# Two tiles taken in turn by halves of the weights, and another order of the first loads

## The chip, the cores and the metric

The kernel runs on one core of a Trainium2 chip. The metric is the device time of the whole program in microseconds (us), as the median of several runs. A core has a matrix engine (TensorE, PE in the rows, with its weight loads as PEld), a vector engine (VectorE, DVE), a scalar engine (ScalarE, ACT), a general engine (GpSimd, POOL) and a sync engine (SyncE, SP). They run side by side and wait for each other by semaphores; each takes its own instructions in order. Here SP issues nearly all DMA transfers, and POOL issues those that store attention's results and those that add what they bring to what is there. SBUF is the memory on the chip from which the engines work, PSUM holds what PE sums up, in banks of 128 x 512 fp32 values, and DRAM is the memory outside.

## What is computed

Three layers follow one another: linear attention with a norm (8 batches, 8 heads, 576 positions, 64 values a head), a first feed-forward layer with squared ReLU, and a second one with g = h·cos(h). The tokens are 8 x 576 = 4608, the model width is 512, the inner width 2048.

```
kv  = einsum('bhsd,bhse->bhde', k, v);  out = einsum('bhsd,bhde->bhse', q, kv)
x   = out / sqrt(mean(out*out, -1) + 1e-6) * g_norm          # heads side by side: 4608 x 512
x   = relu(x @ w_in)**2 @ w_out                              # first layer
out = (h * cos(h)) @ w2_out, with h = x @ w2_in              # second layer
```

The weights come as 64-bit numbers, and the kernel builds its own 32-bit values from their two words. Every large product is made of three: a value is split into a high part that PE's fast fp32 form keeps exactly and a low part, and high·high, high·low and low·high are added.

## The kernel before

**Tiles and chunks.** The first layer is done in two ways. One half of its inner width (8 weight blocks of 128, `NH`) goes through `layer_in` and `layer_out` for 9 tiles of 512 tokens (`NTILE`); this is the first stage, to about 495 us. The other half of the first layer and the whole second one follow in `run_slots`, in a scheme with seven products in place of eight on blocks of four, and its results are added to those of the first stage. A chunk is one tile with one weight block: `layer_in(t, f)` makes the 128 x 512 first products in 12 matmuls (L383), `act_relu2` squares and splits them (ACT at L392, L394 and L397, DVE at L398), and `layer_out(t, f)` makes 12 matmuls (L420) into four accumulators `acc0` to `acc3`, one for each 128 output columns, over all weight blocks of the tile. `layer_out` comes two chunks behind `layer_in` (`LAG`). Behind a tile's last weight block `evict` copies the four accumulators to SBUF, two by ACT (L406) and two by DVE (L408), and SP stores the pairs to DRAM in `p_d` (L409). The order of chunks is a plain list (L682): all eight blocks of tile 0, then all eight of tile 1, and so on.

**Attention runs beside the chunks.** For each batch: five loads of k and v (`load_kv`, L247), 80 small matmuls (`kv_mm`, L259), a copy to `kvx` (L272), and then eight units, two for each of four pairs of heads: `att_a` (PE at L292 for the first two batches, in full fp32, at L296 for the others; ACT at L303 and L304), `att_b` (PE at L318 or L320, ACT at L323 and L325), `att_c` (DVE at L333, L334, L335) and, for the first two batches, `att_d`, which writes the split result straight into the tiles 0 and 1 (ACT at L352, DVE at L353). Tile 0 is tokens 0 to 511, all from batch 0; tile 1 is 512 to 1023, the rest of batch 0 and most of batch 1. `att_e` stores the results, from where the later tiles are loaded.

**Weights.** `load_w` brings one half of a block (half 0 is of w_in, half 1 of w_out; 512 KB) and `conv_steps` turns it into high and low parts: DVE at L111, L113, L116, L122, L125 and L206, ACT at L112 and L205. Eight blocks make 16 conversions.

**What sets the order.** Each job has a position on a line that counts chunks (`at`, `run_jobs`), negative ones come before the first chunk. The 16 conversions stand at -14 to -13.7 (blocks 0 and 1), from -2.2 in steps of 0.7 (blocks 2 to 5) and from 4 in steps of 0.8 (blocks 6 and 7). Batch 0's units start at -13, one for each step of 1, batch 1's at -3 in steps of 0.8. `att_b`, `att_c` and `att_d` follow at 1.5 behind. The jobs are issued in the order of their positions, and a planner under the language then orders each engine's instructions by its own reckoning of when they are ready, with that order as the priority. Loads go ahead in streams: the first are issued by hand (L898 to L903): two weight halves, five tiles of k and v, one weight half, four of q, one weight half; after that each conversion issues the load of a later one (`Stream.place`), as soon as a buffer is free.

**Sums.** In the second stage, `load_sum` (L588) loads the first stage's results from `p_d` as the start of the first layer's sums, and `drain_product` adds the second half's products from PSUM (L670).

Of the kernel before, what the change touches and what calls it, by code (L numbers as in the profile page):

```python
# [8 lines left out]
F32 = mybir.dt.float32  # L9
# [4 lines left out]
ALU = mybir.AluOpType  # L14
PSUM = bass.MemoryType.PSUM

P = 128
# [5 lines left out]
def kernel(  # L23
# [15 lines left out]
    nc = tc.nc  # L39
    NT, DM = out.shape  # L40
    NKC = DM // P
    NF = wA.shape[0]
    NH = NF // 2
# [3 lines left out]
    NRAW = 4  # L47
# [5 lines left out]
    TOK = 512  # L53
    NTILE = NT // TOK
# [11 lines left out]
    dram = ctx.enter_context(tc.tile_pool(name="dram", bufs=1, space=bass.MemoryType.DRAM))  # L66
# [4 lines left out]
    zerob = cpool.tile([P, 1], F32, name="zerob")  # L71
    expb = cpool.tile([P, 1], F32, name="expb")

    x_d = [dram.tile([P, NKC, S], F32, name=f"x_d{b}") for b in range(B)]
    p_d = [dram.tile([P, NKC, TOK], F32, name=f"p_d{t}") for t in range(NTILE)]
    y_d = [dram.tile([P, 2, NKC, ht], F32, name=f"y_d{t0}") for t0, ht in TILES]
    first_pair = (NP, 0)
    groups_of = [range(NP // 2), range(NP)]
# [25 lines left out]
    wts = {}  # L104
# [60 lines left out]
    def conv_steps(kind, m, f, i):  # L165
        raw = raws.pop((kind, m, f, i))
        if kind in ("pair", "seven", "pairs"):
            n = 2 * P if kind == "pairs" else P
            w, e = words(raw, [P, 4, n])
# [7 lines left out]
            if where:  # L177
                size = 1024 // n
# [20 lines left out]
        w, e = words(raw, [P, DM])  # L199
        wf = as32(w[:])  # L200
        value(raw, wf, w, e)
        if i == 0:
            wts[m, f] = [w_p.tile([P, 2, DM], F32R, tag="w", name=f"w{x}") for x in "hl"]
        h, l = (x[:, i, :] for x in wts[m, f])
        nc.scalar.copy(out=h, in_=wf)  # L205
# [192 lines left out]
        nc.vector.tensor_tensor(out=l, in0=g, in1=as32(h[:]), op=ALU.subtract)  # L398
        return h, l

    def evict(t, i, acc):
        if i % 2 == 0:
            evs[t, i // 2] = ev_p.tile([P, 2, 512], F32, tag="ev", name="ev")
        both = evs[t, i // 2]
        if i % 2 == 0:
            nc.scalar.copy(out=both[:, 0, :], in_=acc)  # L406
        else:
            nc.vector.tensor_copy(out=both[:, 1, :], in_=acc)  # L408
            nc.sync.dma_start(out=p_d[t][:, i - 1:i + 1, :], in_=both)  # L409

    def layer_out(t, f):
        wh, wl = (x[:, 1, :] for x in wts[0, f])
        gh, gl = gs.pop((t, f))
        for i in range(NKC):
            if f == 0:
                accs[i] = bank_tile(f"acc{i}")
            o = accs[i]
            cs = slice(i * P, (i + 1) * P)
            for n, (a, m) in enumerate(((wh, gh), (wh, gl), (wl, gh))):
                nc.tensor.matmul(  # L420
                    o, a[:, cs], m[:], start=(f == 0 and n == 0), stop=(f == NH - 1 and n == 2), skip_group_check=True
                )
            if f == NH - 1:
                evict(t, i, o)


    slots = [(m, t, q) for m in range(2) for t in range(len(TILES)) for q in groups_of[m]]
# [155 lines left out]
    def load_sum(k, d, j):  # L583
        m, t, q = slots[k]
        t0, ht = TILES[t]
        sums[m, t, d, j] = e = w_p.tile([P, 2, 512], F32, tag="w", name="sum")
        for b, s0, done, size in pieces(t0 + j * ht, ht, TOK):
            nc.sync.dma_start(out=e[:, :, done:done + size], in_=p_d[b][:, 2 * d:2 * d + 2, s0:s0 + size])  # L588

    def s_block(k, i):  # L590
        m, t, q = slots[k]
# [87 lines left out]

    chunks = [(t, f) for t in range(NTILE) for f in range(NH)]  # L682
    nA0 = NTILE * NH
    nAtt = 49
    LAG2 = 1.25
# [35 lines left out]
        return [(kind, m, p, i) for p in ps for i in range(2)]  # L721

    w_items, w_at = [], []
    for fs, n, step in ((range(2), -14, 0.1), (range(2, 6), -2.2, 0.7), (range(6, NH), 4, 0.8)):
        new = [("one", 0, f, i) for f in fs for i in range(2)]
        w_items += new
        w_at += [n + step * k for k in range(len(new))]
    for new, n0, n1 in (
# [12 lines left out]
    late_stream.place([pos(n) for n in (0.95, 2.5, 3.25, 4.5, 6.4, 8.3, 11.3)], 0, lead=0.5)  # L741

    kv_stream = Stream(load_kv, kv_mm, [(b, c) for b in range(B) for c in range(NSC)])
    starts = [(-13, 1), (-3, 0.8)] + [(-3 + 7 * (b - 1), 7 / (2 * NKC)) for b in range(2, B)]
    kv_stream.place([s0 - 0.5 for s0, _ in starts for c in range(NSC)], 0)
    q_items = [(b, p) for b in range(B) for p in range(NKC)]
    q_next = NKC
# [138 lines left out]
    with ExitStack() as early:  # L886
        pools["ps"] = early.enter_context(tc.tile_pool(name="ps0", bufs=1, space=PSUM))
        def right(name, bufs):
            return early.enter_context(tc.tile_pool(name=name, bufs=bufs, side="right"))

        right("pad", 1).tile([P, 56], F32, name="pad")
        ev_p, pools["raw"] = right("ev", 2), right("conv", 2)
        x_p, g_p, pools["t"] = (right(n, b) for n, b in (("x", XB), ("g", 3), ("tmp", 8)))
        with tc.tile_pool(name="att", bufs=1, side="right") as att_p:
            kvx = [att_p.tile([P, NKC, P], F32, tag=f"kvx{b}", name=f"kvx{b}") for b in range(2)]
            for x in kvx:
                nc.gpsimd.memset(x, 0.0)
            w_stream.advance(2)  # L898
            kv_stream.advance(KVB)
            w_stream.advance(1)  # L900
            for p in range(NKC):
                load_q(0, p)
            w_stream.advance(NRAW - 3)  # L903
            run_jobs(-1)
            banks.update(o=["o", "acc3"], ss=["ss"], l=["l0", "l1"])
            run_chunks(0, nAtt)
        pools["x"] = ctx.enter_context(tc.tile_pool(name="xb", bufs=13, side="left", reuse_waits="tile"))
        banks["l"] = ["l0", "l1", "o", "ss"]
        run_chunks(nAtt, nA0)
        for c in chunks[-LAG:]:  # L910
            layer_out(*c)
# [48 lines left out]
```

## Time and profile before

| what | value |
| --- | --- |
| median of 3 runs | 1559.48 us (1559.1 to 1560.09) |
| the profiled execution's own time | 1560.63 us |
| its span, first to last instruction | 1558.8 us |
| PE busy | 1533.3 us, 98% of the span |
| DVE busy | 1294.2 us, 83% |
| ACT busy | 1077.1 us, 69% |
| POOL busy | 109.8 us, 7% |
| DMA | 426.71 MB, 274 GB/s on average |

The profile is of one execution. An engine's busy time is the union of its instructions' records. A matmul's record is longer than the time to the next matmul's start, since they are pipelined. In the rows, L383 is line 383 of the kernel, `out<-in` names the tiles written and read, and a bracket tells how long the engine was idle before and what ended that. The granted clock of TensorE was 1.00 in all stretches read here.

### The profile page before, as it was taken

The numbers are of one execution on the slowest core, as the hardware profiler recorded it, in microseconds if no ns is written. First come the engines' busy times: TensorE is split into PE (matmuls) and PEld (weight loads), VectorE is DVE, ScalarE is ACT, GpSimd is POOL, SyncE is SP. The second block draws the span as 40 slices with busy tenths as digits, with TensorE's granted clock in tenths as the row PEclk, the third lists the DMA queues.
The fourth block names the chain that finished last, engine by engine and source line by source line (L and its number), as shares of the span: only waits on it lengthen the run. The fifth ranks groups of instructions, "written<-read, shape, count | busy, mean of one in ns | idle before, by whom it ended". The sixth has DMA issues, their size and how long they took to land.

```text
span 1558.8 us, 24668 instructions
## 1 busy us (share of the span) xinstructions
PE 1533.3 (98%) x9104; PEld 1345.9 (86%) x9104; DVE 1294.2 (83%) x1743; ACT 1077.1 (69%) x1529; POOL 109.8 (7%) x173
## 2 busy tenths in 40 slices
PE   6999999999999999999999999999999999999998
PEld 4677777778888888888998899999999999999998
DVE  6987888888886899989889979867986788779777
ACT  6977777775444765656556777776777677777775
POOL 1112111110000000000000000000000000000001
PEclk9999999999999999999999999999999999999999
DMA  9748889777678989898999788887888789999996
GB/s 337 270 149 244 276 283 275 222 214 214 206 226 298 325 253 367 299 380 267 364 339 372 265 281 255 249 285 215 254 247 284 215 247 273 298 326 292 301 311 171
DMA packets 222295, 426.71 MB, mean 274 GB/s; under 512 B 18016, under 2 KB 138080, under 8 KB 222176
## 3 DMA queue, kind: packets, MB, share of 16 engines
q1 hardware_dynamic: 210400, 390.13, 72.8%
q0 software_dynamic: 11616, 35.01, 10.6%
q8 instruction: 73, 1.20, 0.3%
q14 instruction: 46, 0.38, 0.1%
q10 hardware_dynamic: 160, 0.00, 0.0%
HBM read 317.72 MB, written 81.79 MB: 256 GB/s over the span
## 4 chain that ended last, share of the span: by engine, by line
PE 87%; DVE 5%; DMA 3%; ACT 2%; issue 2%; SPq 0%; POOL 0%; DVEq 0%; ACTq 0%; POOLq 0%
PE FB L509 16%; PE FA L509 16%; PE SA L642 16%; PE SB L642 15%; PE acc L420 11%; PE l L383 9%; PE o L383 1%; PE ss L383 1%; DMA xraw<-x_d 1%; DMA sum<-part 1%; PE o L259 1%; DMA ws_d<-raw 1%; DMA kvld<-in_kv 1%; DVE gl L619 1%; PE l L259 1%
## 5 line engine op out<-in xcount | busy, mean ns | idle before, releaser
L509 PE MATMUL FB<-xh,wi 128*128 128x512 f32 (+1 forms) x840 | 301.4, 370 | 0.0
L509 PE MATMUL FA<-xh,wi 128*128 128x512 f32 (+1 forms) x840 | 301.4, 370 | 0.0
L642 PE MATMUL SB<-ws,gh 128*128 128x256 f32 x1008 | 233.0, 280 | 0.6 <-ACT part L667 0.6
L642 PE MATMUL SA<-ws,gh 128*128 128x256 f32 x1008 | 233.2, 280 | 0.0
L642 PEld LDWEIGHTS SA<-ws,gh 128*128 128x128 f32 x1008 | 183.7, 188 | 12.8 <-issue 0.5
L642 PEld LDWEIGHTS SB<-ws,gh 128*128 128x128 f32 x1008 | 183.3, 188 | 12.6 <-ACT part L667 0.8
L509 PEld LDWEIGHTS FB<-xh,wi 128*128 128x128 f32 x840 | 157.2, 188 | 9.6
L509 PEld LDWEIGHTS FA<-xh,wi 128*128 128x128 f32 x840 | 157.1, 188 | 9.0
L642 PE MATMUL SB<-ws,gl 128*128 128x256 f32 x504 | 141.2, 280 | 0.3 <-DVE gl L619 0.3
L642 PE MATMUL SA<-ws,gl 128*128 128x256 f32 x504 | 141.2, 280 | 0.1
L619 DVE TENSOR_TENSOR gl<-y,gh 128x1024 fp32r<-128x1024 f32 (+1 forms) x98 | 109.5, 1118 | 36.7 <-ACT gh L618 36.7
L668 POOL DMA_DIRECT2D sum<-part x54 | 47.2, 874 | 1136.2 <-DMA wi_d<-raw 530.6
L579 DVE SCALAR_TENSOR_TENSOR y<-y,h 128x1024 f32<-128x1024 f32 (+1 forms) x79 | 88.2, 1117 | 46.1 <-ACT y L575 45.8
L561 ACT ACTIVATE y<-h,zerob 128x1024 int32<-128x1024 f32 (+1 forms) x79 | 84.1, 1065 | 48.7 <-DVE h L535 48.1
L420 PE MATMUL acc<-gh,wh 128*128 128x512 f32 x288 | 113.5, 396 | 1.6 <-ACT og L304 1.6
L420 PE MATMUL acc<-gl,wh 128*128 128x512 f32 x288 | 112.9, 392 | 0.0
L420 PE MATMUL acc<-gh,wl 128*128 128x512 f32 x288 | 112.6, 391 | 0.0
L509 PE MATMUL FA<-xl,wi 128*128 128x512 f32 (+1 forms) x300 | 111.0, 370 | 0.0
L509 PE MATMUL FB<-xl,wi 128*128 128x512 f32 (+1 forms) x300 | 110.9, 370 | 0.0
L571 ACT ACTIVATE y<-y 128x1024 f32<-128x1024 f32 (+1 forms) x79 | 77.2, 978 | 36.5 <-DVE y L565 36.4
L642 PE MATMUL SA<-gh,ws 128*128 128x512 f32 (+1 forms) x280 | 100.8, 369 | 0.9 <-ACT wh L192 0.7
L642 PE MATMUL SB<-gh,ws 128*128 128x512 f32 (+1 forms) x280 | 100.5, 369 | 0.9 <-DMA ws<-ws_d 0.9
(174 smaller groups left out, 3814.0 us busy)
## 6 DMA issues: line engine op xcount, KB each, us to landing
wi<-wi_d SPq DMA_DIRECT2D x210, 512.0 KB, 6.5
ws<-ws_d SPq DMA_DIRECT2D x210, 512.0 KB, 5.9
sum<-part POOLq DMA_DIRECT2D x33, 512.0 KB, 7.3
kvld<-in_kv SPq DMA_DIRECT2D x32, 512.0 KB, 7.8
ws_d<-raw SPq DMA_DIRECT2D x24, 448.0 KB, 4.4
q<-in_qT SPq DMA_DIRECT2D x32, 288.0 KB, 5.2
p_d<-ev SPq DMA_DIRECT2D x18, 512.0 KB, 3.9
raw<-in_wA SPq DMA_DIRECT2D x16, 512.0 KB, 7.3
```

What stands on the lines that cost most here:

```text
L259: nc.tensor.matmul(kv_ps[b][r, p, r], t[:n, 0, head], t[:n, 1, head], start=(c == 0 and p == 0), stop=(c == NSC - 1), skip_group_check=True,)
L383: nc.tensor.matmul(ps, a[:, 0, cs], m[:], start=(c == 0 and k == 0), stop=(c == NKC - 1 and k == 2))
L420: nc.tensor.matmul(o, a[:, cs], m[:], start=(f == 0 and n == 0), stop=(f == NH - 1 and n == 2), skip_group_check=True)
L509: nc.tensor.matmul(ps[:, pp, :], a, b, start=(n == 0 and (i in (0, 2) or i == 1 and not seeded(k))), stop=(n == 5), skip_group_check=True,)
L561: nc.scalar.activation(out=y.bitcast(I32), in_=hs[k, b], func=AF.Identity, bias=zerob)
L571: nc.scalar.activation(out=y, in_=y, func=AF.Sin, scale=math.pi)
L579: nc.vector.scalar_tensor_tensor(out=y, in0=y, scalar=-2.0 * math.pi, in1=hs.pop((k, b)), op0=ALU.add, op1=ALU.mult)
L619: nc.vector.tensor_tensor(out=l, in0=src, in1=as32(h), op=ALU.subtract)
L642: nc.tensor.matmul(ps[:, b, :], lhs, rhs, start=(n == 0 and (m == 0 or b % 2 == 0) and i in (0, 1, 2)), stop=(n == 5), skip_group_check=True,)
L668: nc.gpsimd.dma_start(out=e, in_=part, accum_op=ALU.add)
```

## The change

The first 16 chunks take the tiles 0 and 1 in turn by halves of the weight blocks: tile 0 with blocks 0 to 3, tile 1 with blocks 0 to 3, tile 0 with 4 to 7, tile 1 with 4 to 7. Since the four accumulators serve one tile at a time, each of the two tiles is emptied behind each half, the first half into `p_d`, the second into the new `p2_d`. Where `load_sum` reads from one of these two tiles, a second transfer, issued by POOL, adds the part from `p2_d` to what the first brought. Blocks 2 and 3 are converted from -5.5 in steps of 0.9, blocks 4 to 7 from 1 in steps of 0.9; batch 1's units start at -4.6. The first loads become: half 0 of block 0, five tiles of k and v, four of q, half 0 of block 1, half 1 of block 0 and half 1 of block 1.

```diff
+    HALVES = 2
+    p2_d = [dram.tile([P, NKC, TOK], F32, name=f"p2_d{t}") for t in range(HALVES)]
...
-        if i == 0:
+        if (m, f) not in wts:
             wts[m, f] = [w_p.tile([P, 2, DM], F32R, tag="w", name=f"w{x}") for x in "hl"]
...
-    def evict(t, i, acc):
+    def evict(t, i, acc, dst):
...
-            nc.sync.dma_start(out=p_d[t][:, i - 1:i + 1, :], in_=both)
+            nc.sync.dma_start(out=dst[t][:, i - 1:i + 1, :], in_=both)
...
+        firsts = (0, NH // 2) if t < HALVES else (0,)
+        lasts = (NH // 2 - 1, NH - 1) if t < HALVES else (NH - 1,)
         for i in range(NKC):
-            if f == 0:
+            if f in firsts:
                 accs[i] = bank_tile(f"acc{i}")
...
-            if f == NH - 1:
-                evict(t, i, o)
+            if f in lasts:
+                evict(t, i, o, p2_d if t < HALVES and f == NH - 1 else p_d)
...
+            if b < HALVES:
+                nc.gpsimd.dma_start(
+                    out=e[:, :, done:done + size], in_=p2_d[b][:, 2 * d:2 * d + 2, s0:s0 + size], accum_op=ALU.add
+                )
...
-    chunks = [(t, f) for t in range(NTILE) for f in range(NH)]
+    chunks = [(t, h * NH // 2 + f) for h in range(2) for t in range(HALVES) for f in range(NH // 2)]
+    chunks += [(t, f) for t in range(HALVES, NTILE) for f in range(NH)]
...
-    for fs, n, step in ((range(2), -14, 0.1), (range(2, 6), -2.2, 0.7), (range(6, NH), 4, 0.8)):
+    for fs, n, step in ((range(2), -14, 0.1), (range(2, 4), -5.5, 0.9), (range(4, NH), 1, 0.9)):
         new = [("one", 0, f, i) for f in fs for i in range(2)]
+        if fs[0] == 0:
+            new.sort(key=lambda x: x[3])
...
-    starts = [(-13, 1), (-3, 0.8)] + [(-3 + 7 * (b - 1), 7 / (2 * NKC)) for b in range(2, B)]
+    starts = [(-13, 1), (-4.6, 0.8)] + [(-3 + 7 * (b - 1), 7 / (2 * NKC)) for b in range(2, B)]
...
-            w_stream.advance(2)
+            w_stream.advance(1)
             kv_stream.advance(KVB)
-            w_stream.advance(1)
             for p in range(NKC):
                 load_q(0, p)
-            w_stream.advance(NRAW - 3)
+            w_stream.advance(NRAW - 1)
```

## Rows read from the trace of the kernel before

**Rows 1.** Windows: length, busy us (instructions) of PE, PEld, DVE, ACT, POOL; clock, DMA.

```profile
22.40:62.30 39.90, 34.19 (x269) 24.73 (x267) 39.06 (x93) 35.24 (x89) 6.73 (x12) 1.00 0.86 301
62.30:80.00 17.70, 17.63 (x85) 13.10 (x86) 17.70 (x38) 16.50 (x38) 1.85 (x3) 1.00 0.75 264
```

**Rows 2.** Windows of one line each (PE, PEld): L259, L292, L318, L383, L420.

```profile
0.00:62.30 62.30, 11.64 (x240) 10.03 (x240) 1.00 0.87 305
0.00:62.30 62.30, 11.88 (x32) 6.93 (x32) 1.00 0.87 305
0.00:62.30 62.30, 9.49 (x26) 5.11 (x26) 1.00 0.87 305
0.00:62.30 62.30, 9.44 (x36) 6.53 (x36) 1.00 0.87 305
0.00:62.30 62.30, 7.22 (x24) 4.32 (x24) 1.00 0.87 305
```

**Rows 3.** Chain that ended last, 0 to 160 us: start, length, engine, tile, line.

```profile
64.25 0.49 PE ss L318 x2
...
85.73 2.76 PE acc L420 x12
...
111.10 2.63 PE l L259 x80
```

**Rows 4.** Timeline of DVE: start, length, engine, line, operation, tiles.

```profile
22.40 0.46 DVE L333 SCALAR_TENSOR_TENSOR m<-ss,r 128x288 f32<-128x288 f32 x1 [0.66 <-ACT r L325]
...
47.41 0.45 DVE L333 SCALAR_TENSOR_TENSOR m<-ss,r 128x288 f32<-128x288 f32 x1
47.78 0.68 DVE L398 TENSOR_TENSOR gl<-g,gh 128x512 fp32r<-128x512 f32 x1
48.38 0.69 DVE L116 SCALAR_TENSOR_TENSOR w<-raw,w 128x512 uint32<-128x512 uint32 x1
48.98 0.69 DVE L122 SCALAR_TENSOR_TENSOR e<-raw,e 128x512 uint32<-128x512 uint32 x1
49.58 0.45 DVE L334 SCALAR_TENSOR_TENSOR m<-m,r 128x288 f32<-128x288 f32 x1
...
50.92 0.42 DVE L111 TENSOR_SCALAR e<-raw 128x512 uint32<-128x512 uint32 x1
51.26 0.42 DVE L113 TENSOR_SCALAR w<-raw 128x512 uint32<-128x512 uint32 x1
```

**Rows 5.** Timeline of PE, the first matmuls of batch 0.

```profile
8.68 1.12 PE L259 MATMUL o<-kvld 128*64 128x64 f32 x16 [8.68 <-DMA kvld<-in_kv]
9.96 1.12 PE L259 MATMUL o<-kvld 128*64 128x64 f32 x16 [0.16 <-DMA kvld<-in_kv]
...
15.35 1.12 PE L259 MATMUL o<-kvld 64*64 64x64 f32 x16 [0.49 <-DMA kvld<-in_kv]
17.41 2.26 PE L292 MATMUL acc<-q,kvx 128*128 128x288 f32 x4 [0.95 <-ACT kvx L272]
```

**Rows 6.** Line L279, 0 to 15 us: the loads of q, issue and landing.

```profile
L279 SPq DMA_DIRECT2D q<-in_qT x4: 327/339/429, 7.7 to 9.9; - x4
...
DMA to landing us min/median/max: 9.3/9.5/9.9
```

**Rows 7.** Lines L406 and L408: count, ns min/median/max, first and last start.

```profile
L406 ACT COPY ev<-acc x18: 565/589/639, 102.4 to 494.2; 128x512 f32<-128x512 f32 x18
L408 DVE COPY ev<-acc x18: 679/684/692, 103.1 to 494.9; 128x512 f32<-128x512 f32 x18
```

**Rows 8.** Lines L588 and L668: landing of sum loads and of accumulating transfers.

```profile
DMA to landing us min/median/max: 5.0/7.7/9.5
DMA to landing us min/median/max: 3.8/7.4/11.8
```

**Rows 9.** Timeline of SP and DVE: first load of a sum and its use.

```profile
489.65 0.37 SPq L588 DMA_DIRECT2D sum<-p_d  x1
526.45 1.22 DVE L670 TENSOR_TENSOR sum<-SA,sum 128x1024 f32<-128x1024 f32 x1
```

More of the change, by code (lines that the diff above doesn't have):

```diff
@@ L420, in layer_out @@
                 nc.tensor.matmul(
-                    o, a[:, cs], m[:], start=(f == 0 and n == 0), stop=(f == NH - 1 and n == 2), skip_group_check=True
+                    o, a[:, cs], m[:], start=(f in firsts and n == 0), stop=(f in lasts and n == 2), skip_group_check=True
                 )
-            if f == NH - 1:
-                evict(t, i, o)
+            if f in lasts:
+                evict(t, i, o, p2_d if t < HALVES and f == NH - 1 else p_d)
     slots = [(m, t, q) for m in range(2) for t in range(len(TILES)) for q in groups_of[m]]
```

## The prediction

> **What bounds the kernel now.** I read the page's busy shares first, then the work on PE by windows, then the chain of waits, and last the single instructions of the first 80 us. PE is busy 98% of the 1558.8 us, so only time in which PE does nothing useful, or new PE work, can move the end. The change adds no matmul. The place to look is the start: from 62.3 to 80 us PE is busy 17.63 of 17.7 us, before that it is not, and DVE is busy 39.06 of 39.9 us from 22.4 to 62.3 and all of the next 17.7 us [rows 1]. So the first 62.3 us are bound by the loads, then by DVE, and from there PE sets the pace.
>
> Busy time overstates PE, because a matmul's record is longer than the step to the next one: twelve of a chunk step by in 2.76 us, two fp32 ones of the attention in 0.49, and the 80 of one batch's k·v in 2.63 [rows 3]. I price the work done by 62.3 us with these steps [rows 2]: 240 k·v matmuls 7.9 us, 32 q·kv and 26 sum-of-squares records 7.8 and 6.4, 36 of L383 8.3, 24 of L420 5.5: 35.9 us. PE has lost 26.4 us by then. 14.8 of them lie before the first q·kv at 17.41 (17.41 less one batch of k·v) [rows 5], 11.6 behind it. That is all that this change can win.
> The rule for reading this is in the Trainium skill, Trainium Kernel Development and Optimization, section Performance Expectations: matmul busy time is a bad measure, since matmuls are pipelined. By busy time PE would lack 5.7 us between 22.4 and 62.3 (39.9 less 34.19) [rows 1], and no gain behind 22.4 could be larger; priced by steps the lack there is larger, and the trace agrees with the rule.
>
> **What DVE has to do.** Steps from one DVE start to the next [rows 4]: 0.37 us for L333 (L334, L335 and L353 have its shape), 0.60 for L398, L116 and L122 (L125 and L206 have their shape), 0.34 for L111 (L113 has its shape). So a converted weight half costs DVE 3.1 us, a unit of attention 1.5, a batch of eight units 12, a chunk 0.6. Check: batch 0 (12), six conversions (18.6), four units of batch 1 (6) and two chunks (1.2) are 37.8, and the start of the next conversion makes it 38.9, against 39.06 busy.
>
> **The order of the chunks.** Before, chunk f of tile 0 needs weight f, that is 6.2 us of DVE for a chunk that costs PE 5.5 (24 matmuls, two times 2.76). After, four weights serve eight chunks, but chunk 4 needs tile 1, that is all of batch 1. I compare the moment T from which PE is no longer short. Before it is 62.3 with chunk 3. After it is chunk 4: by then DVE has to do, counted from the first unit, batch 0 (12), the second halves of weights 0 and 1 (6.2), weights 2 and 3 (12.4), batch 1 (12) and three chunks (1.8): 44.4 us, and 0.8 idle as in the row. Weights 4 to 7 are placed from position 1 on and needed at 8 to 11; they fill DVE behind T.
>
> **The first loads.** k·v of batch 0 now stands behind one weight half, not two. Tiles of 512 KB land 1.28 us apart (8.68 and 9.96), but the last lands at 15.35, 2.2 us later than that pace gives (8.68 plus 3.5 times 1.28) [rows 5]. So k·v ends 1.3 to 3.5 us earlier. The q tiles land 9.3 to 9.9 us after issue [rows 6], the first issued at 7.72, so at about 17.2; they now stand ahead of two weight halves that were ahead of them, 2.6 us. I take 1.6 us for the first q·kv, near the low end, since one weight less in the queue is the part that a row shows. SP issues the same loads; only their order differs.
> A page's rule is stricter here: the Trainium skill, DMA: Bandwidth & Descriptors, section Queues, rings and completion order, says that on each engine descriptors are consumed in ring order. By it later loads can't have caused the slow last tile, and the gain is 1.28 us. The trace does not bear it out alone: the pace of the first two tiles agrees, the last tile at 15.35 is later than the rule and that pace give. By the rule the forecast would be 0.3 us later.
> The price: the second half of weight 0 was converted while DVE had nothing else to do, before 16 us. After, it lands with the last loads and its 3.1 us fall into the full stretch; they are in the 44.4.
> So the full stretch begins at 22.4 (the first unit's L333 [rows 4]) less 1.6, at 20.8, and T = 20.8 + 44.4 + 0.8 = 66.0.
>
> **What PE can do by T.** Without batch 1's last units PE has k·v of three batches 7.9, all exact attention (64 records) 15.7, the first products of chunks 0 to 3 11.0, the second of 0 to 2 8.3: 42.9 us. On top can come chunk 3's second product (2.8) and three quarters of chunk 4's first (2.1), which need no last unit: 47.8. Below, PE may lag in its order, since ACT is also busy 35.24 of 39.9 us [rows 1]: with 40 the gain would be 0.4. I take 44.1, a quarter of the way from 42.9 to 47.8, because ACT has so little room. Lost: 66.0 − 44.1 = 21.9, against 26.4: 4.5 us won. The ends are 0.4 and 8.2 (66.0 less 47.8 is 18.2 lost).
>
> **Four more accumulators to empty, twice.** Two tiles are now emptied twice: four more copies of 0.59 us on ACT and four of 0.68 on DVE [rows 7]. All lie between chunks 5 and 10, where after T weights and attention leave DVE and ACT room; PE meets an accumulator again one chunk later, with 2.76 us of first products between. I take nothing; if PE waited for each copy, it would be 4 × 0.59 + 4 × 0.68 = 5.1 us at most.
> **The second sums.** Four more stores of 512 KB, and four accumulating loads on POOL's queue, which has nothing queued then. The first sum is loaded at 489.65 and used at 526.45 [rows 9]. The load lands in 5.0 to 9.5 us, an accumulating transfer in 3.8 to 11.8 [rows 8]: at the worst 489.65 + 9.5 + 11.8 = 511, 15 us ahead. The chain sum load, accumulate, drain is longer, but covered; without the cover one transfer (7.4) would come on the path. Value: nothing. Traffic of 4 MB on 427 is no term.
>
> **Sum.** The profiled execution took 1560.63 us, 1.15 above the median of 1559.48. 1560.63 − 4.5 = 1556.1 on its own scale, 1555.0 on that of the median.
>
> **Rivals.**
> 1. Chunk 4 comes late (slower). Batch 1 now has to be finished first, and if conversions of weights 4 and 5, placed at 1.0, 1.9 and 2.8, stand on DVE's or ACT's queue ahead of the last units (placed at 2.5 by their split), each moves T by 3.1 us. What PE can do without tile 1 ends at 45.6 us (7.9 + 15.7 + 11.0 + 11.0), so it decides at T = 45.6 + 26.4 = 72.0. Two such conversions bring 72.2, no change; with a third T is 75.3 and the kernel is 3.3 us slower, 1562.8; with a fourth 6.4. For it: before, DVE had converted weight 4's first half and begun the next with four units of batch 1 still open. Against: they are placed later now than before.
> 2. No change. PE is limited by all of DVE's work up to the last weight, not by that ahead of chunk 4, and PE's in-order queue with one free first-product bank makes of the earlier weights nothing: what is won at the loads (1.6) is about paid by the conversion that moved into the full stretch (3.1), with 1.5 us of the order's gain left to make up for it: 1559.5. For it: DVE has no idle time to 80 us [rows 1]. Against: from 62.3 PE was full although DVE was too, so not all of DVE's work has to precede.
> 3. The second sums or the extra copies reach PE: 5 to 7 us at most, 1560 to 1562 with the gain kept. Against it the 15 us above.
> 4. It does not do what it says: the order on the engines comes from a planner, which may place the conversions as before; this lies within case 2.
>
> **How the numbers follow.** The forecast case has 0.61, of whose span (1551.3 to 1559.1) about five sixths lie more than 3.1 us below; 0.2% of 1559.5 is 3.1, about what a measurement of this kernel can tell from no change. Case 1 has 0.16, case 2 with 4 0.19, case 3 0.04. Faster: 0.61 × 5/6 = 0.51. Same: the other 0.10 with case 2 and a little of case 1, 0.32. Slower: 0.17. The range goes from 1550.5 (the forecast's end with the larger gain at the loads) to 1561.5 (case 2 and the mild part of case 1).
>
> **What would show it.** First q·kv at about 15.8 instead of 17.41; DVE full from about 21; chunk 4, the first on tile 1, at 64 to 68 us, with PE without gaps behind it; no wait of PE on L406 or L408, none for the sums near 526. It is wrong if PE waits again behind 70 us, if chunk 4 starts behind 72, or if the gain does not stand before 80 us.

## The result: slower by 8 us, and the profile after

The changed kernel takes 1568.26 us in the median of six runs (1565.98 to 1570.51), before in the same runs 1559.93 (1559.1 to 1560.57): a ratio of 1.0053, 95% interval 1.0043 to 1.0062. The forecast was 1555.0. The profiled execution took 1570.51 us, the longest of the six; its span is 1568.7 (before 1558.8). The first matmul of the second stage starts at 502.6 us, before at 494.7; behind it the kernel takes 1066.1 and 1064.1 us. So 7.9 of the 9.9 us stand in the first stage and 2.0 in the second.

Line numbers are two higher than before up to `evict`, four from the loop in `layer_out` on and eight behind `load_sum`: L335 is [rows 4]'s L333, L385 is L383, L424 is L420, L678 is L670. Rows of a run have the lines of the kernel that it starts from, with what its own edit adds.

The windows that answer to [rows 1] (length; busy us of PE, PEld, DVE, ACT, POOL; clock; DMA):

```profile
22.40:62.30 39.90, 28.65 (x157) 20.04 (x156) 37.89 (x89) 31.57 (x80) 6.14 (x11) 0.75 0.82 283
62.30:80.00 17.70, 17.70 (x147) 13.57 (x145) 16.19 (x39) 13.06 (x31) 2.64 (x5) 0.99 0.41 134
```

PE is full from 62.3 us, as before. Up to there it is busy 28.65 us in place of 34.19, and the granted clock of the first row is 0.75, where it was 1.00. The same lines as in [rows 2], in their order, up to 62.3 us:

```profile
0.00:62.30 62.30, 9.31 (x160) 8.17 (x160) 0.84 0.84 291
0.00:62.30 62.30, 11.75 (x30) 6.78 (x30) 0.84 0.84 291
0.00:62.30 62.30, 10.63 (x24) 5.69 (x24) 0.84 0.84 291
0.00:62.30 62.30, 13.41 (x34) 8.12 (x35) 0.84 0.84 291
0.00:62.30 62.30, 0.00 (x0) 0.00 (x0) 0.84 0.84 291
```

One batch of k·v fewer, four fp32 records fewer, no second product at all. Priced as in the prediction this is 5.3 + 7.3 + 5.9 + 7.8 = 26.3 us of work, so 36.0 us are lost, against 26.4. The busy time of L385 is larger than before (13.41 for 34 matmuls, 9.44 for 36), and that is no work: each took longer.

Why, DVE's timeline shows (start, length, what, idle before and its end):

```profile
8.62 0.69 DVE L208 TENSOR_TENSOR wl<-w,wh 128x512 fp32r<-128x512 f32 x1 [0.68 <-ACT wh L207]
21.78 0.46 DVE L335 SCALAR_TENSOR_TENSOR m<-ss,r 128x288 f32<-128x288 f32 x1 [12.47 <-ACT r L327]
...
22.64 0.42 DVE L113 TENSOR_SCALAR e<-raw 128x512 uint32<-128x512 uint32 x1
...
24.89 0.43 DVE L113 TENSOR_SCALAR e<-raw 128x512 uint32<-128x512 uint32 x1
...
26.16 0.43 DVE L113 TENSOR_SCALAR e<-raw 128x512 uint32<-128x512 uint32 x1
...
31.65 0.46 DVE L355 TENSOR_TENSOR xl<-xo,xh 128x288 fp32r<-128x288 f32 x1
32.02 0.46 DVE L335 SCALAR_TENSOR_TENSOR m<-acc,r 128x288 f32<-128x288 f32 x1
```

DVE does one conversion, then nothing for 12.47 us, and then three conversions (three L113) at once, with the first unit of attention between them; the second unit's L335 comes at 32.02, before's L333 at 26.49. Before, three conversions lay ahead of attention, the third of them from 16.34 to 21.74, and one behind its first unit. DVE's timeline before:

```profile
16.34 0.43 DVE L111 TENSOR_SCALAR e<-raw 128x512 uint32<-128x512 uint32 x1 [3.73 <-DMA raw<-in_wA]
...
21.05 0.69 DVE L206 TENSOR_TENSOR wl<-w,wh 128x512 fp32r<-128x512 f32 x1 [1.54 <-ACT wh L205]
...
26.49 0.82 DVE L333 SCALAR_TENSOR_TENSOR m<-acc,r 128x288 f32<-128x288 f32 x2
```

PE's waits in the changed kernel, and what came behind them (the list of waits, then PE's timeline):

```profile
PE acc L320 <- DVE m L335: 4.0, 1, 4.0
PE acc L294 <- ACT og L306: 3.0, 1, 3.0
PE l L385 <- ACT r L394: 2.3, 1, 2.3
PE l L385 <- ACT xh L354: 1.6, 1, 1.6
```

```profile
27.79 0.75 PE L294 MATMUL acc<-q,kvx 128*128 128x288 f32 x2 [2.96 <-ACT og L306]
32.53 2.76 PE L320 MATMUL acc<-sq,ones 128*128 128x288 f32 x4 [3.99 <-DVE m L335]
...
56.91 0.80 PE L385 MATMUL l<-xh,wh 128*128 128x512 f32 x1 [2.27 <-ACT r L394]
57.50 0.63 PE L385 MATMUL l<-xl,wh 128*128 128x512 f32 x1
57.93 0.63 PE L385 MATMUL l<-xh,wl 128*128 128x512 f32 x1
58.35 0.63 PE L385 MATMUL l<-xh,wh 128*128 128x512 f32 x1
```

Before, PE's waits from 18 to 35 us were these two:

```profile
26.59 0.75 PE L292 MATMUL acc<-q,kvx 128*128 128x288 f32 x2 [0.88 <-ACT og L304]
...
29.52 0.74 PE L383 MATMUL l<-xh,wh 128*128 128x512 f32 x2 [1.21 <-ACT xh L352]
```

After 57.50 the steps are 0.43 us where a chunk's matmul takes 0.23 (2.76 by 12 [rows 3]): PE came back from its waits at half its clock. The changed kernel by tens of us, then two of the same stretches before:

```profile
10.00:20.00 10.00, 6.94 (x63) 5.28 (x60) 0.00 (x0) 2.34 (x6) 0.00 (x0) 1.00 1.04 341
20.00:30.00 10.00, 5.58 (x19) 3.57 (x17) 8.19 (x18) 8.45 (x20) 0.75 (x1) 0.93 0.80 299
30.00:40.00 10.00, 7.33 (x83) 5.27 (x85) 10.00 (x27) 6.66 (x18) 1.88 (x4) 0.56 0.93 318
40.00:50.00 10.00, 9.38 (x49) 7.00 (x43) 8.96 (x21) 8.59 (x24) 1.38 (x3) 1.00 0.97 332
50.00:60.00 10.00, 6.46 (x15) 4.18 (x16) 10.00 (x24) 7.47 (x19) 1.94 (x3) 0.63 0.68 222
```

```profile
30.00:40.00 10.00, 9.46 (x107) 7.19 (x106) 9.69 (x29) 8.73 (x26) 3.25 (x6) 1.00 1.03 413
50.00:60.00 10.00, 8.24 (x72) 5.53 (x72) 10.00 (x23) 7.31 (x17) 1.08 (x2) 1.00 0.64 204
```

### The profile page after: what moved, and what is told of

Same layout as the page of the kernel before. It is cut to its first block, busy times and chain, and to the rows that moved or that the text cites. A ratio compares the mean times of both kernels' runs of the same rounds, so it can differ in the third digit from the quotient of the medians.

```text
span 1568.7 us, 24691 instructions
## 1 busy us (share of the span) xinstructions
PE 1537.3 (98%) x9104; PEld 1350.6 (86%) x9104; DVE 1295.6 (83%) x1747; ACT 1077.6 (69%) x1533; POOL 112.5 (7%) x177
## 4 chain that ended last, share of the span: by engine, by line
PE 88%; DMA 4%; DVE 4%; issue 2%; ACT 1%; SPq 0%; POOL 0%; DVEq 0%; ACTq 0%; POOLq 0%
PE SA L650 15%; PE SB L650 15%; PE FB L513 15%; PE FA L513 14%; PE acc L424 13%; PE l L385 11%; DMA ws<-ws_d 1%; PE o L385 1%; PE ss L385 1%; PE o L261 1%; DMA kvld<-in_kv 1%; DVE gl L627 1%; DMA sum<-part 1%; DMA wi<-wi_d 1%; DMA wi_d<-raw 1%
## 5 line engine op out<-in xcount | busy, mean ns | idle before, releaser
L424 PE MATMUL acc<-gh,wh 128*128 128x512 f32 x288 | 113.3, 395 | 0.0
L424 PE MATMUL acc<-gl,wh 128*128 128x512 f32 x288 | 112.9, 392 | 0.0
L424 PE MATMUL acc<-gh,wl 128*128 128x512 f32 x288 | 112.6, 391 | 0.0
L385 PE MATMUL l<-xh,wh 128*128 128x512 f32 x244 | 99.0, 407 | 3.9 <-ACT r L394 2.3
```

The lines of the kernel that those rows point to most:

```text
L385: nc.tensor.matmul(ps, a[:, 0, cs], m[:], start=(c == 0 and k == 0), stop=(c == NKC - 1 and k == 2))
L424: nc.tensor.matmul(o, a[:, cs], m[:], start=(f in firsts and n == 0), stop=(f in lasts and n == 2), skip_group_check=True)
```

## The experiments

Theory A: the loss is DVE work that moved from idle time into the stretch in which DVE is full. Rivals: the alternation or its positions; the second sums; the granted clock. The letters of the rivals stand in the expectations. Columns of the table: the median; the ratio to before, run on the same chip beside it; the time of the one execution that was profiled. The last three columns are of that execution alone: the us lost by 80 us, by the prediction's prices (and 0.65 us for each eight of the small products with which batch 2 begins, the step from the first of them at 65.83 to what follows at 66.48 before); PE's idle us from 18 to 80; the slow time there, which is the busy time times (1 less the granted clock), us by us.

| run | median us | ratio [95%] | profiled us | lost by 80 | idle | slow |
| --- | --- | --- | --- | --- | --- | --- |
| before | 1559.93 | 1 | 1560.63 | 26.8 | 5.8 | 0.0 |
| the changed kernel | 1568.26 | 1.0053 [1.0043, 1.0062] | 1570.51 | 36.9 | 11.3 | 7.2 |
| b_loads_after | 1566.30 | 1.0036 [1.0023, 1.0048] | 1566.75 | 34.9 | 10.2 | 6.2 |
| a_loads_before | 1562.25 | 1.0015 [1.0006, 1.0024] | 1562.96 | 29.3 | 8.3 | 1.7 |
| a_conv_late | 1567.12 | 1.0044 [1.0029, 1.0059] | 1568.42 | 35.5 | 9.8 | 5.2 |
| h_two_first | 1568.96 | 1.0059 [1.0045, 1.0073] | 1567.22 | 35.5 | 8.8 | 7.5 |
| l_dve_3us | 1562.31 | 1.0018 [1.0009, 1.0027] | 1562.74 | 30.0 | 8.2 | 1.7 |
| m_dve_6us | 1565.83 | 1.0041 [1.0028, 1.0054] | 1563.42 | 32.1 | 10.3 | 0.0 |
| g_weights_first | 1559.63 | 1.0001 [0.9992, 1.0011] | 1559.77 | 27.1 | 5.1 | 0.0 |
| f_warm | 1573.69 | 1.0085 [1.0067, 1.0104] | 1569.05 | - | 8.3 | 4.8 |
| c_alt_only | 1563.44 | 1.0022 [1.0012, 1.0031] | 1563.45 | 29.9 | 8.1 | 0.0 |
| e_pos_only | 1564.62 | 1.0030 [1.0018, 1.0042] | 1566.65 | 31.2 | 7.7 | 5.3 |
| n_batch1_only | 1566.28 | 1.0040 [1.0027, 1.0053] | 1565.04 | 31.5 | 6.6 | 1.7 |
| d_split_only | 1562.37 | 1.0019 [1.0010, 1.0029] | 1561.89 | 27.1 | 6.1 | 2.2 |
| i_split_sum_early | 1569.38 | 1.0062 [1.0049, 1.0075] | 1569.38 | 28.6 | 5.9 | 3.0 |
| j_alt_sum_early | 1571.62 | 1.0075 [1.0063, 1.0088] | 1568.85 | 29.3 | 7.4 | 1.5 |
| k_alt_weights_first | 1569.27 | 1.0066 [1.0053, 1.0078] | 1572.52 | 28.9 | 6.1 | 1.7 |

### The loads: alone, and without them

**a_loads_before**, the changed kernel with the loads of before:

```diff
-        if fs[0] == 0:
-            new.sort(key=lambda x: x[3])
...
-            w_stream.advance(1)
+            w_stream.advance(2)
             kv_stream.advance(KVB)
+            w_stream.advance(1)
...
-            w_stream.advance(NRAW - 1)
+            w_stream.advance(NRAW - 3)
```

> The changed kernel with the first loads (and the order of the first four conversions) of the kernel before. Theory A, the loads: in the changed kernel DVE stood still from 9.3 to 21.8 us, and three conversions (9.2 us) then stood ahead of attention; with the old loads one of them is done before 13 us and another from about 16 us, PE's waits of 3.0 and 4.0 us near 27.8 and 32.5 go, and the time is 1555 to 1560 us. Theory B, the alternation and the earlier batch 1: the loads are not the cause, the time stays at 1565 to 1570 us.

**b_loads_after**, the counterpart: before, with this edit the other way round and nothing else of the change.

> The kernel before with only the first loads (and the order of the first four conversions) of the changed one. Theory A: DVE stands still to about 22 us here too, the conversions bunch up and the time is 1565 to 1570 us. Theory B: first loads are worth less than 2 us either way, 1558 to 1562 us.

The loads alone make before slower by 0.36%, 5.6 us; without them the change costs 0.15%, 2.3 us. With the loads alone PE waits 3.42 us up to 27.7 and 3.42 up to 32.5, as in the changed kernel. So the larger part of the loss comes with the loads. It is not all of it: a_loads_before, at 1562.25, is above what theory A expected. The edit has two parts, the order of the loads and that of the first four conversions, and no run has one without the other.

### Where the conversions go

**a_conv_late**, the changed kernel with the conversions of blocks 0 and 1's second halves placed among batch 0's last units:

```diff
+    w_at[2:4] = [-7.0, -6.2]
```

> The changed kernel with the second halves of blocks 0 and 1 converted at positions -7.0 and -6.2, behind the start of attention, in place of -13.8 and -13.7; the loads stay. Theory A, where the bunching is what hurts: DVE does attention first, PE's waits of 3.0 and 4.0 us near 27.8 and 32.5 go or shrink to 1 us, 1560 to 1564 us; DVE's idle time to 21.8 us stays. Theory B: 1565 to 1570 us, no change.

The early waits went: 22.2 us are lost by 40, against 27.3 in the changed kernel. But 34.6 are by 60, against 34.8, and the clock is 0.50 between 50 and 60. A miss for theory A as worded, no measurable gain: DVE had the same to do, only later.

**h_two_first**, the changed kernel with two weight halves loaded first, so that one of the moved conversions returns to idle time:

```diff
-            w_stream.advance(1)
+            w_stream.advance(2)
...
-            w_stream.advance(NRAW - 1)
+            w_stream.advance(NRAW - 2)
```

> The changed kernel with one edit: the first loads are two weight halves (half 0 of blocks 0 and 1), keys and values, q, two weight halves; so the first half of block 1 can be converted again while DVE has nothing else to do, before attention. Theory A (the loss is DVE's idle time before 21.8 us, with one more conversion, 3.1 us, put into its full stretch): 3 us come back, some 1565 us in the median against 1568 of the changed kernel, DVE busy about 7 to 8 of the ten us from 10 to 20, only two conversions between 22 and 33 us, and PE's wait for m at 32.5 shorter than 3.99. Rival B (the start of attention decides; it comes 1.3 us later with one more weight ahead): 1.3 us of that is paid back, 1566 to 1567. Rival C (the conversions' place in the full stretch is all that matters, and the planner still mixes them into attention's first units): no difference, 1568.

A miss for theory A. DVE does convert two halves by 12.7 us and waits 9.19 us, not 12.47, PE's idle time falls by 2.5 us; but the slow time stays (clock 0.63 from 30 to 40, 0.72 from 50 to 60), and the median does not move.

**l_dve_3us** and **m_dve_6us**, before with useless DVE work of the same size in the same stretch; loads, chunks and positions are untouched (5 and 10 subtractions, 0.60 us each):

```diff
+    def extra():
+        h, l = (x[:, 1, :] for x in wts[0, 1])
+        t = temp([P, DM], F32, "extra")
+        for _ in range(5):
+            nc.vector.tensor_tensor(out=t, in0=as32(l), in1=as32(h), op=ALU.subtract)
+
+    at(-13.65, extra)
```

> Before, with five more DVE subtractions of 128x512 (0.60 us each, 3.0 us) of block 1's second half into a tile that nobody reads, right behind the last of the first four conversions; loads, chunks and positions are before's. Theory A (each us of DVE work added to its full stretch ahead of 62 us costs PE a us): 1562.9 in the median against 1559.9. Rival G (DVE's work costs only where PE has to wait long enough for its granted clock to fall; 3 us do not): less than 1.5 us, 1560 to 1561.3. Rival H (the loss came with the loads and not with DVE's work): no difference.

> The same with ten subtractions, 6.0 us, about what the new loads moved into the full stretch (two conversions of 3.1 us). Theory A: 1565.9. The run with the new loads alone stood 5.6 us above before, so with A and only DVE's work behind it this run stands there too. Rival G: PE's waits near 30 us reach 3 to 4 us and the granted clock falls to 0.5 behind them as in the changed kernel; more than 6 us, 1566 to 1568, that is more than twice the run above. Rival H: no difference.

0.18% and 0.41% are 2.8 and 6.4 us for 3.0 and 6.0 us of DVE work: one for one in the medians, as theory A said. The six are what two conversions (6.2) would be, and the loads alone cost 5.6. Rival H falls, and so does the first half of rival G, less than 1.5 us for the shorter work. But the profile of m_dve_6us is that of its shortest execution, 1563.42 us, 3.8 above before's median. In its windows DVE is full and ACT has only 5.10 in the first row, while the clock stays at 1.00:

```profile
30.00:40.00 10.00, 7.85 (x99) 5.53 (x100) 10.00 (x24) 5.10 (x13) 1.08 (x2) 1.00 1.03 413
40.00:50.00 10.00, 8.48 (x32) 5.12 (x31) 10.00 (x26) 10.00 (x29) 2.14 (x4) 1.00 0.65 223
50.00:60.00 10.00, 6.91 (x30) 4.96 (x28) 10.00 (x23) 7.26 (x15) 1.08 (x2) 1.00 0.61 200
```

The other four executions took 1565.26 to 1568.12 us, and their mean granted clock was 0.996 to 0.999. So DVE work added to its full stretch costs PE time without any slow clock: PE's idle time grows by 4.5 us and the execution by 3.8 for 6.0 us of work. What the median has beyond that came with a lower clock, and the second half of rival G is not refuted.

**g_weights_first**, before with all four halves ahead of k, v and q:

```diff
-            w_stream.advance(2)
+            w_stream.advance(NRAW)
             kv_stream.advance(KVB)
-            w_stream.advance(1)
...
-            w_stream.advance(NRAW - 3)
```

> The kernel before with all four first weight halves loaded ahead of k and v and q. Theory A, what counts is that DVE has conversions to do while k, v and q land: attention starts 1.3 to 2.6 us later, but another conversion or two (3.1 to 6.2 us) leave the full stretch, 1557 to 1560 us. Rival, the start of attention counts: 1561 to 1563 us.

One more conversion (3.1 us) in idle time, and attention 2.5 us later: the first q·kv came at 19.95 for 17.41, DVE's first L333 at 24.95 for 22.40. No difference in the time, as theory A expected. DVE's list is not all; the start of attention is the other side of it. (The expectation of k_alt_weights_first below takes 1.3 us for this later start; it was 2.5.)

### The clock

**f_warm**, the changed kernel with 32 matmuls of 128x512 that nobody reads, four in each of batch 0's units:

```diff
+    def warm():
+        w = wts[0, 0][0][:, 0, :]
+        t = bank_tile("l1")
+        for _ in range(4):
+            nc.tensor.matmul(t, w[:, :P], w, start=True, stop=True)
...
+            if b == 0:
+                at(n + 0.9, warm)
```

> The changed kernel with 32 matmuls of 128x512 added whose results nobody reads, in batch 0's attention, so that PE has something to do where it waits; 20 of them stand among the attention matmuls where PE waited 3.0 and 4.0 us. If the fall of the granted clock (0.5 to 0.64 from 28 to 40 us) costs time of its own, it stays at 1.0 there and the kernel gains 2 to 4 us on the changed one, 1563 to 1566 us. If DVE sets the pace there whatever PE's clock, the clock changes and the time stays at 1566 to 1570 us.

The granted clock was 1.00 from 20 to 30 and 0.83 from 30 to 40 (0.56 in the changed kernel), yet PE waited for the same L335 until 32.0 us, and the kernel was not faster. It is slower, with four runs far apart (1569.05 to 1576.08), and the added matmuls cost PE time of their own, so this run tells little of how much the slow clock takes; it only shows that DVE's order, and not the clock, holds PE until 32 us.

The single executions say more, since each has its mean granted clock on record. Within one kernel those with the lower clock are longer: m_dve_6us 1563.42 at 1.000 and 1568.12 at 0.996, e_pos_only 1562.54 at 1.000 and 1566.65 at 0.996, b_loads_after 1564.20 at 0.998 and 1566.75 and 1566.84 at 0.994. With (1 less the clock) times 1565 us as an execution's slow time, a straight line through each of the three gives 0.4 to 0.6 us more for one us of it, an estimate. A longer wait could make both, so that the clock is the cause is not shown.

### The alternation and its positions

**c_alt_only**: the changed kernel with the loads and the conversions' positions of before, and batch 1 from -3.7. **e_pos_only**: before with the new positions of conversions and batch 1. **n_batch1_only**: before with batch 1 moved alone. The last one's edit:

```diff
-    starts = [(-13, 1), (-3, 0.8)] + [(-3 + 7 * (b - 1), 7 / (2 * NKC)) for b in range(2, B)]
+    starts = [(-13, 1), (-4.6, 0.8)] + [(-3 + 7 * (b - 1), 7 / (2 * NKC)) for b in range(2, B)]
```

> The tiles taken in turn, with the kernel before's loads and its positions of the conversions; batch 1 starts at -3.7 (the latest at which tile 1 is there for chunk 4). Theory A: no bunch, so at most 3 us off the kernel before, 1556 to 1563 us. Theory B, if it is the alternation: chunk 4 is late, 1565 to 1570 us; if it is the earlier batch 1 and weights: 1558 to 1562 us.

> The kernel before with one thing of the changed one: the positions (blocks 2 and 3 from -5.5, blocks 4 to 7 from 1, batch 1 from -4.6), with the old chunk order, loads and no second emptying. Theory A, what is left of the loss without the loads (2 us) comes from putting batch 1 ahead of the chunks: 1561 to 1564 us. Rival, it comes from the alternation: 1559 to 1561 us here.

> Before, with batch 1's units from -4.6 instead of -3, nothing else. All the new positions without the alternation cost 5 us. If batch 1 alone makes that (its units take DVE and ACT from the conversions that before's chunk order wants next): 1563.5 to 1565, with PE waiting for weights or for ACT's r at 45 to 60 us. If the weights' positions make it: within 1 us of before.

The three medians lie 0.4, 0.6 and 1.3 us above what theory A, or the first case of the last one, expected. Batch 1 earlier by 1.6 positions costs before's chunk order 0.40%, 6.2 us; with the weights' new positions it is 0.30%, and the second stage starts at 500.4 us; with the alternation too (a_loads_before) it is 0.15%, and the second stage starts at 495.6, 0.9 behind before. By these two profiles the alternation earns 4.8 us in the first stage, but that of e_pos_only is its longest execution of six; the medians of the two kernels are 2.4 us apart. The earlier batch 1 that it needs costs more than that in before's chunk order; what it costs within the alternation was not measured. In c_alt_only, with batch 1 less early, the second stage starts at 496.5, 1.8 behind before, without any slow time. The waits, of batch 1 alone and of a_loads_before:

```profile
PE l L383 <- ACT r L392: 3.7, 2, 2.4
```

```profile
PE l L385 <- ACT r L394: 3.0, 1, 3.0
```

It is the first product of a chunk that waits, for `act_relu2` to free its bank. In a_loads_before it waits until 50.42; on ACT the squaring stands behind a conversion, for which ACT itself waits for DVE, and behind steps of attention's units:

```profile
47.20 0.62 ACT L207 CAST wh<-w 128x512 fp32r<-128x512 f32 x1 [1.05 <-DVE w L127]
...
49.39 0.48 ACT L306 ACTIVATE og<-acc,gcol 128x288 f32<-128x288 f32 x1
49.78 0.59 ACT L394 ACTIVATE r<-l 128x512 f32<-128x512 f32 x1
```

Around chunk 4 PE does not wait: in the changed kernel and in a_loads_before it has no idle time from 60 to 80 us.

### The second sums

**d_split_only**: before with the two emptyings and the second sums, the chunks in plain order. **i_split_sum_early**: the same, but the parts are added when the second part is emptied, so the second stage has no accumulating loads. **j_alt_sum_early**: a_loads_before with that edit. **k_alt_weights_first**: the same with g_weights_first's loads. The edit that adds the parts early, in the last three:

```diff
+            if dst is p2_d:
+                nc.gpsimd.dma_start(out=both, in_=p_d[t][:, i - 1:i + 1, :], accum_op=ALU.add)
             nc.sync.dma_start(out=dst[t][:, i - 1:i + 1, :], in_=both)
...
-            nc.sync.dma_start(out=e[:, :, done:done + size], in_=p_d[b][:, 2 * d:2 * d + 2, s0:s0 + size])
-            if b < HALVES:
-                nc.gpsimd.dma_start(
-                    out=e[:, :, done:done + size], in_=p2_d[b][:, 2 * d:2 * d + 2, s0:s0 + size], accum_op=ALU.add
-                )
+            src = p2_d if b < HALVES else p_d
+            nc.sync.dma_start(out=e[:, :, done:done + size], in_=src[b][:, 2 * d:2 * d + 2, s0:s0 + size])
```

> The kernel before with one thing of the changed one: the tiles 0 and 1 are emptied twice, with the second store and the accumulating loads, while the chunks keep their old order (tile 0 then tile 1), and loads and positions are the old ones. Theory A, copies and sums hidden: 1559 to 1561 us. Rival: the copies hold up PE, or the accumulating loads the second stage, 1562 to 1565 us.

> Before's order, loads and positions, with tiles 0 and 1 emptied twice, but the two parts are added as soon as the second is there: an accumulating transfer brings the first part from DRAM onto the second part's tile ahead of its store, at 60 to 150 us, and the sums at the start of the second stage are single loads as before. Theory D (the 1.8 us that splitting alone cost in the second stage come from the accumulating transfers that run at its start, together with the stores of the last accumulators, for which DVE and then PE wait): 1560.0 us, within 0.8 of before, and no wait of PE on L545 (h<-FB), which was 2.3 us. Rival E (they come from the other addresses and stores, or from the emptying): 1562.4 as with splitting alone.

> The changed kernel with before's first loads and order of the first four conversions, and with the parts of tiles 0 and 1 added early as in the run above. With before's loads alone it was 2.0 us above before, of which 0.9 stood in the first stage and 1.1 in the second. Theory D: the 1.1 go, about 1561.0, that is 0.9 above before or no measurable difference. Rival E: 1562.2. In either case no gain over before: the alternation earns back what the earlier positions cost, not more.

> As the run above, with all four weight halves loaded ahead of keys, values and q. With before's chunks this order put one more conversion into DVE's idle time and started attention 1.3 us later, and moved nothing. Theory A (what DVE has to do in its full stretch ahead of the tile that is wanted next decides): one conversion less, 3.1 us less the later start of 1.3: 1.8 us below the run above, about 1559.2, level with before or a little under it. Rival F (attention's start decides where tile 1 is wanted early): 1.3 us above the run above, 1562.3.

Splitting alone costs 0.19%, 3.0 us, the rival's range. In its profile the first stage ends as before (494.2 us), the second takes 1065.9 us. There DVE and then PE wait (DVE's timeline, then PE's):

```profile
501.75 0.69 DVE L115 TENSOR_SCALAR w<-raw 128x1024 uint32<-128x1024 uint32 x1 [3.46 <-DMA p_d<-ev]
...
503.62 1.22 DVE L543 TENSOR_TENSOR h<-FB,m 128x1024 f32<-128x1024 f32 x1
```

```profile
504.90 0.50 PE L513 MATMUL FB<-xh,wi 128*128 128x512 f32 x1 [2.33 <-DVE h L543]
```

The store of the last accumulators lands late, up to 6.5 us from issue (before 3.5), a conversion on DVE waits for it, L543 stands behind that conversion, and PE behind L543. In the changed kernel the wait on the store is 1.93 us and PE's 0.81, less than half of the 2.0 us by which its second stage is longer; the first accumulating load is issued beside that store:

```profile
503.00 0.96 POOL L594 DMA_DIRECT2D sum<-p_d  x1 [133.41 <-PE acc L424]
```

Without these loads (i, j, k) the second stage takes 1064.0, 1063.6 and 1063.8 us, DVE's wait is at most 0.39 and PE's is gone, as theory D says. It is not so in every kernel that has them: a_loads_before takes 1065.4 without a wait of PE, a_conv_late and h_two_first 1063.8 and 1063.4. In these two the first of the loads is issued at 503.39 and 502.79, as close to that store, and DVE waits 0.40 and 0.28 us. Kernels without second sums at all lie between 1062.9 and 1064.4, one execution each. So that these loads make the store late fits i, j and k; when they do and when not stays open.

The early sums' price was larger than their gain, and all three medians missed their expectation by 9 to 11 us. Between 130 and 220 us PE is idle for 4.8, 5.8 and 5.8 us in the three, for 0.8 before and for 0.0 in d_split_only and a_loads_before. The store of an early sum waits for its accumulating transfer on SP, which takes its transfers in order and so issues no load in that time: 16.0 us in all in i_split_sum_early, 13.3 and 13.8 in the other two (the list of SP's waits, then SP's timeline, then PE's):

```profile
SPq L413 <- DMA ev<-p_d: 16.0, 4, 6.6
```

```profile
165.62 0.38 SPq L198 DMA_DIRECT2D ws_d<-wh  x1
172.61 0.33 SPq L413 DMA_DIRECT2D p_d<-ev  x1
```

```profile
194.30 0.40 PE L322 MATMUL ss<-sh,ones 128*128 128x288 f32 x1 [3.73 <-DMA raw<-in_wA]
```

That SP's stop is what PE later waits for is read from the order on SP, not shown by a run. By 140 us j and k have lost as much as a_loads_before, to 0.5 us: one more conversion in idle time did not help the alternation either.

No version beat before.

## Why the prediction was wrong

Two steps failed, and the runs split the miss between them. The gain of 4.5 us was 6.0 from the order of the chunks, by the moment T, less 1.5 for the loads (3.1 less 1.6). Measured were a loss of 2.3 without the new loads (a_loads_before) and one of 5.6 with them alone (b_loads_after), together 7.9, against 8.3 for the whole change. From 4.5 won to 7.9 lost the forecast missed by 12.4 us: 8.3 of them (6.0 and 2.3) lie with the order of the chunks and what it needs, the new positions and the second sums, and 4.1 (5.6 less 1.5) with the loads.

**The cost of the first loads: mis-sized.** The prediction let one conversion's 3.1 us fall into the full stretch, the second half of weight 0. Two fell: the first half of block 1 was the third load before, ahead of q, and DVE converted it from 16.34 on while it waited for attention; its rows, from 16.34 to 21.74, lie just ahead of those that were read. It now comes behind q. The list of 44.4 us lacks its 3.1. Against these 6.2 us stands the earlier start, taken as 1.6 us: the first q·kv came at 16.79, 0.62 us earlier, and DVE's first L335 0.62 earlier (21.78 for 22.40). Together 5.6 us worse than before, which is what the loads alone cost; the prediction had 1.5. The agreement is in part luck: at a full clock 6.0 us of DVE work cost 3.8 (m_dve_6us), b_loads_after has 6.2 us of slow time besides, and giving one conversion back to idle time gained nothing (h_two_first).

**The head start's bounds.** The end of k·v was to come 1.3 to 3.5 us earlier. Its first tile came 1.48 us earlier, the last only 0.63 (14.72 for 15.35 [rows 5]). By the rule of the Trainium skill (DMA: Bandwidth & Descriptors, Queues, rings and completion order) that descriptors are consumed in ring order, and with the 1.28 us between the first tiles, all of them had to gain 1.28. The trace does not agree: the last tile stands 3.0 us behind the pace of 1.28 a tile from the first (7.20 and 3.5 times 1.28), before 2.2, so the load less ahead did not reach the end of k·v in full.

**The moment T: the larger failure.** It was to be chunk 4, at 66.0. Chunk 4 starts at 76.88, past the 72 that was named as a sign of being wrong, and PE had had no wait since 56.91 without it, at last with second products of tile 0 that had been held back. In a_loads_before PE has no wait from 50.42 to 80 and has still lost 2.5 us more than before by 80. So chunk 4's moment sets nothing in these two: PE loses its time earlier, where a first product waits for ACT or an attention matmul for DVE.

**What PE can do by T.** 44.1 us of work by 66 were taken; the changed kernel had 26.3 by 62.3, and with PE full from there about 30 by 66. The sum of all that needs no last unit is not what comes in order through one bank and a busy ACT: rival 2's reason, which the prediction gave one chance in five and only for no change.

**Batch 1 earlier** was in the list with its 12 us of DVE work, but not priced by what it keeps waiting on ACT. In before's chunk order it costs 6.2 us by itself. The alternation does save conversions ahead of the eight chunks; that batch 1's units pay this back on DVE and ACT is read from the waits above, and how much it is stays open.

**Rival 1** named the place (slower, conversions ahead of attention's units) but wrong batch and wrong weights: not blocks 4 and 5 ahead of batch 1, but blocks 0 and 1 ahead of batch 0.

**Evictions at nothing: right.** The copies (22 on each engine for 18) take 0.59 and 0.68 us as in [rows 7], and only PE's weight loads wait for one of them, 0.4 us.

**The second sums at nothing: wrong by some 2 to 3.** The changed kernel's second stage is 2.0 us longer, and d_split_only costs 3.0. The sums are there in time; their first drains at 535 to 545 wait for nothing. What the step left out is whom the transfers may delay: the store of the last accumulators and the conversion behind it, which is where PE's 0.8 us of waiting come from; the rest of the 2.0 stays open.

**The clock** was read as 1.00 throughout and kept out of the forecast. It fell to half behind some of PE's waits, and 7.2 us of slow time stand in the changed kernel. How much of the 8.3 us by which the kernel is slower this is stays open: m_dve_6us lost 3.8 us without it and 5.6 to 8.5 in its executions with a lower clock, b_loads_after 5.6 with it, and in h_two_first the idle time won came out as no gain while the slow time stayed. Lost time and idle time do not add up to a price for it, since some of the slow work would have waited anyway.

## What to carry to other kernels

Before a load is moved, list every instruction that an engine did in its idle time because of the old order, each one by its row; the engine that is full later pays for each that falls out, here 2.8 us for 3.0, and for 6.0 us 3.8 at a full clock and 6.4 in the median. A profile shows one execution: whether it stands for the median depends on where its time and its clock lie among the others. A bound by the moment at which some tile is ready holds only if the profile shows an engine waiting for that tile; where it waits for a bank or for a helper engine's queue, doing other work earlier takes from that queue. Of an extra transfer ask not only whether it lands in time, but which transfer beside it now lands later and who waits for that one.

## What was unexpected of the hardware

The granted clock went from 1.00 to 0.50, from TensorE's 2.4 to its 1.2 GHz, behind waits of 2.96 and 3.99 us with one pair of attention's matmuls between them: the 80 matmuls of a batch of k·v then took 3.70 us instead of 2.63 [rows 3]. The length of the wait alone does not tell. In the profile of m_dve_6us five waits of 1.2 to 3.0 us left the clock at 1.00, the longest of them the first row below; in h_two_first a shorter one, the second row, had it at 0.50 from 28 us on.

```profile
57.89 0.50 PE L420 MATMUL acc<-gh,wh 128*128 128x512 f32 x1 [2.97 <-ACT og L304]
```

```profile
27.19 1.32 PE L294 MATMUL acc<-q,kvx 128*128 128x288 f32 x2 [2.73 <-ACT og L306]
```
